# A Fourier filter with a gated feed-forward layer on one core: the gated layers worked unit by unit, PSUM dealt out as four, two and two banks, and another order of the work on ACT and DVE

## The chip, the core and the metric

The kernel runs on one core of one Trainium2 chip. The core has five engines with instruction queues of their own, each worked strictly in the order in which it was written: PE (matrix products, with PEld for the loading of weights), DVE, ACT and POOL (elementwise work), and SP, which here only issues DMAs. [...] The metric is the device time of one execution in microseconds (us), as the median of the runs shown. "Profiled execution" is one further run, from which the trace comes.

## The reference, cut to what matters

```python
X = np.fft.rfft(x, axis=1)                  # x: 8 batches, 3136 positions, 256 channels, fp32
Y = X * (filt_r + 1j * filt_i)[None, :, :]
x = np.fft.irfft(Y, n=3136, axis=1)
h = np.maximum(x @ w_in, 0.0)               # w_in 256 x 1024
hp = h padded by one position on either side
conv = sum(conv_w[k] * hp[:, k:k + 3136, :] for k in range(3))   # three taps per hidden channel
out = (h * 1.0 / (1.0 + np.exp(-conv))) @ w_out                  # w_out 1024 x 256
```

So each batch goes through a forward transform, a product with a filter, a backward transform, a matrix product with ReLU, a convolution of three taps, a sigmoid gate, and a second matrix product.

## The kernel before, in words

**The transform of a batch** is split as 3136 = 112 x 28 and runs in four kinds of operation, called "1" to "4" here as in the code, each of them 14 times per batch (two of the 28 columns at a time). "1" and "3" are products with a table that differs from column to column (`by_column`, L231), whose result ACT copies out of PSUM (`store`, L226) and SP sends to a scratch buffer in HBM. "2" is a product with a fixed matrix (`second`, L235), whose result DVE takes out of PSUM while multiplying it by the filter (`filt`, L244 to L246, three instructions of DVE), after which POOL adds the two halves (L247); the sum `z` is the input of a "3". "4" is the last product (`fourth`, L255, eight matmuls), whose result DVE copies to SBUF (L572), ACT rounds to the reduced format that PE takes at full rate (`y`, high part, L145), and POOL subtracts to have the low part (L151). Every "2" and "4" first loads what "1" and "3" wrote to HBM.

**The gated layers** are tiled by 448 positions (seven to a batch, 56 in all; the after-code calls such a tile a unit) and by 128 hidden channels (eight blocks `f`). For one tile and one block there are: `inner` (six matmuls of 450 columns, high and low parts, into a PSUM bank `ps_h`, L176 to L178); `relu` on ACT, in place in PSUM (L426), and the centre tap on ACT, from PSUM into an SBUF tile `t` (L428); the two outer taps on DVE, PSUM and `t` into `t` (`conv`, L433 and L434); the sigmoid on ACT (L438) and the product with h on DVE (`gate`, L439); the rounding of the gated value on ACT (L145) and its low part on POOL (`split_g`, L151); and `project`, three matmuls of 256 columns for each 128 positions, which add up over the eight blocks in PSUM banks `po` (L459 to L461). When the last block has been added, DVE copies `po` to SBUF (`evacuate`, L475) and SP stores it.

**What sets the order.** Batch 0's whole transform and batch 1's "1" come first, while the weights are converted (stage 1). Then stage 2 runs through 448 steps, one for each tile and block, by a loop in which everything on PE, ACT, DVE and POOL is issued in the order in which it is written. In step m stand the inner product of item m, the elementwise work of items m-1 to m-3, and the projection of item m-6. A table `plan` says in which steps one (or two) of the transform operations of the following batches stand. In the loop before, the operation is multiplied in the middle of the step on PE, and its result is taken out of PSUM at the very end of the same step on ACT or DVE (`transformed`):

```python
for op in ops[0:1]: transform(op)      # PE, behind inner(m)
project(m - 6); relu(m - 1); conv(m - 1); gate(m - 2); split_g(m - 3); evacuate(m - 6)
for op in ops: transformed(op)         # ACT, DVE, POOL
```

Before, tiles are worked in pairs of 896 positions with the two halves taking turns (seven groups of 128 positions to a pair: four in the first half, three in the second), so that four banks of `po` fill together; three banks serve `ps_h`, and one serves all transform operations (`ps_t`).

Of the kernel before, what the change touches and what calls it, by code (L numbers as in the profile page):

```python
# [124 lines left out]
def tile_fft_filter_gated_ffn(  # L125
# [18 lines left out]
    def hi_act(dst, src):  # L144
        nc.scalar.activation(dst, src, AF.Copy)  # L145
# [4 lines left out]
    def lo_pool(dst, src, hi):  # L150
        nc.gpsimd.tensor_tensor(out=dst, in0=src, in1=hi.bitcast(F32), op=ALU.subtract)  # L151
# [23 lines left out]
    def mm3(ps, wh, wl, rh, rl, start=True, stop=True, **kw):  # L175
        nc.tensor.matmul(ps, lhsT=wh, rhs=rh, start=start, stop=False, **kw)  # L176
        nc.tensor.matmul(ps, lhsT=wh, rhs=rl, start=False, stop=False, **kw)  # L177
        nc.tensor.matmul(ps, lhsT=wl, rhs=rh, start=False, stop=stop, **kw)  # L178
# [37 lines left out]
    def pair(q):  # L216
        return slice(2 * q, 2 * q + 2)
# [39 lines left out]
    def as_y(p):  # L257
        return p.rearrange("p (k c a) -> p k c a", c=2, a=N1)
# [150 lines left out]
    hs, ts, gs, pos = {}, {}, {}, {}  # L409

    def at(m):

        return (m // 16, m // 2 % NF, m % 2) if 0 <= m < 16 * (B * S // CH) else None

    def inner(j, f, i):
        ps = ps_h.tile([128, 512], F32, name="ps_h")[:, 0:SUB + 2]
        fs = slice(128 * f, 128 * f + 128)
        b, u = divmod(2 * j + i, NSUB)
        us = slice(u * SUB, u * SUB + SUB + 2)
        for k in range(KT):  # L420
            mm3(ps, wi[0][:, k, fs], wi[1][:, k, fs], ys[b][0][:, k, us], ys[b][1][:, k, us], start=k == 0, stop=k == KT - 1)
        hs[j, f, i] = ps

    def relu(j, f, i):
        h = hs[j, f, i]
        nc.scalar.activation(h, h, AF.Relu)  # L426
        t = wp.tile([128, SUB], F32, name="t", bufs=4)
        nc.scalar.activation(t, h[:, 1:SUB + 1], AF.Copy, scale=cw[:, 1, f:f + 1])  # L428
        ts[j, f, i] = t

    def conv(j, f, i):
        h, t = hs[j, f, i], ts[j, f, i]
        nc.vector.scalar_tensor_tensor(out=t, in0=h[:, 0:SUB], scalar=cw[:, 0, f:f + 1], in1=t, op0=ALU.mult, op1=ALU.add)  # L433
        nc.vector.scalar_tensor_tensor(out=t, in0=h[:, 2:SUB + 2], scalar=cw[:, 2, f:f + 1], in1=t, op0=ALU.mult, op1=ALU.add)  # L434

    def gate(j, f, i):
        h, t = hs.pop((j, f, i)), ts[j, f, i]
        nc.scalar.activation(t, t, AF.Sigmoid)  # L438
        nc.vector.tensor_mul(t, h[:, 1:SUB + 1], t)  # L439

    def split_g(j, f, i):
        t = ts.pop((j, f, i))
        if i == 0:
            gs[j, f] = [wp.tile([128, 2 * SUB], F32R, name=f"g{h}", bufs=3) for h in range(2)]
        gh, gl = (g[:, i * SUB:i * SUB + SUB] for g in gs[j, f])
        hi_act(gh, t)
        lo_pool(gl, t, gh)

    def project(j, f, i):
        gh, gl = gs[j, f]  # L450
        if f == 0 and i == 0:
            pos[j] = [ps_o.tile([128, 512], F32, name=f"po{k}") for k in range(4)]
        po = pos[j]
        tiles = range(4) if i == 0 else range(4, NT)
        for t in tiles:
            o = po[t // 2][:, t % 2 * D:t % 2 * D + D]
            sl = slice(128 * t, 128 * t + 128)
            first, last = f == 0 and t % 2 == 0, f == NF - 1
            nc.tensor.matmul(o, lhsT=gh[:, sl], rhs=wo[0][:, f], start=first, stop=False, skip_group_check=True)  # L459
            nc.tensor.matmul(o, lhsT=gh[:, sl], rhs=wo[1][:, f], start=False, stop=False, skip_group_check=True)  # L460
            nc.tensor.matmul(o, lhsT=gl[:, sl], rhs=wo[0][:, f], start=False, stop=last, skip_group_check=True)  # L461

    def evacuate(j, f, i):
        if f < NF - 1:
            return
        po = pos[j]
        end = j == B * S // CH - 1
        for k in (0, 1) if i == 0 else (2, 3):
            n = min(2, NT - 2 * k)
# [6 lines left out]
            nc.sync.dma_start(out=outv[j][:, 2 * k:2 * k + n], in_=ot[:, 0:n])  # L476

    NH = 16 * (B * S // CH)
    plan = {}

    def put(m, kind, b, q):
        plan.setdefault(m, []).append((kind, b, q))

    early = {}
    for t in range(1, B):
        w, n = (NF * NSUB * (t - 1), 49) if t % 2 else (NF * NSUB * (t - 1) - 7, 63)
        at2 = 4 if t == 1 else 0 if t % 2 else 10
        late = range(at2 + 34, n - 1)
        taken = set()
        for q in range(NP):  # L490
            at4 = late[q * len(late) // NP]
            taken |= {at2 + 2 * q, at2 + 3 + 2 * q, at4}
            put(w + at2 + 2 * q, "2", t, q)
            put(w + at2 + 3 + 2 * q, "3", t, q)
            put(w + at4, "4", t, q)
        free = [s for s in range(n if t % 2 else n - 4) if s not in taken]
        for q in range(early.get(t, NP), NP):
            put(w + free.pop(0), "1", t, q)
        if t + 1 < B:
            early[t + 1] = min(NP, len(free))  # L500
            if not t % 2:
                free = sorted(free + free[:NP - len(free)])
                early[t + 1] = NP
# [6 lines left out]
    got_in, got_table, got_filter, got_z, banks = {}, {}, {}, {}, {}  # L510

    stored = {("1", 1): NP}

# [45 lines left out]
        if kind == "4":  # L559
            fourth(ps, r)  # L560

    def transformed(op):
        kind, b, q = op
        ps = banks.pop(op)
        if kind in "13":
            store(tp, kind, b, q, ps, 3, "st")
            stored[kind, b] = stored.get((kind, b), 0) + 1
        if kind == "2":
            got_z[b, q] = filt(ps, q, got_filter.pop(op))
        if kind == "4":  # L570
            v = tp.tile([128, 2, D], F32, name="z", bufs=3).rearrange("p j d -> p (j d)")[:, 0:4 * N1]
            nc.vector.tensor_copy(v, ps[:, 0:4 * N1])  # L572
            yh, yl = y_slices(b, pair(q))
            hi_act(yh, as_y(v))
            lo_pool(yl, as_y(v), yh)

    with tc.manual_schedule(engines=COMPUTE):
        for m in range(NH + PLAG):
            ops = plan.get(m, [])
            if a := at(m):  # L580
                inner(*a)
            for op in ops[0:1]:
                transform(op)
            if a := at(m - PLAG):
# [58 lines left out]
```

## Time and profile before

| | us |
|---|---|
| median of 3 runs | 1829.6 (1828.79 to 1830.1) |
| profiled execution | 1823.64 |
| its span, first to last instruction | 1821.9 |
| PE busy in the span | 1586.1 (87%) |
| DVE busy | 1242.6 (68%) |
| ACT busy | 1179.6 (65%) |
| POOL busy | 819.7 (45%) |

The mean granted clock of PE is 0.972. A busy PE is not a PE at its peak, since matmuls overlap and their ends are modelled; the distance from one matmul's start to the next one's is the better measure. Stage 1 ends at about 152 us, where the first `inner` starts; the 448 steps fill the rest. Since each step has exactly two instructions of line L176, the number of these in a stretch of time gives its number of steps. The last 56 steps (batch 7) have no transform work.

### The profile page before, as it was taken

How to read it: one execution, taken by the hardware profiler on the slowest of the kernel's cores; microseconds unless marked ns; L12 is line 12 of the kernel's file. 1: busy time of each engine (PE TensorE's matmuls, PEld its weight loads, DVE VectorE, ACT ScalarE, POOL GpSimd, SP SyncE). 2: the span in 40 equal slices, each digit the busy share in tenths (PEclk: the TensorE clock that was granted, in tenths of full speed). 3: DMA queues.
4: the chain of work that ended last, by engine and by line, in shares of the span. 5: the costliest groups of instructions: out<-in, count | busy, mean ns of one | idle time of the engine just before them, and what ended most of it. 6: DMA issues, size and time to landing. Idle time of an engine off the chain costs nothing. (4 is left out here: it accounts for less than half of the span.)

```text
span 1821.9 us, 27328 instructions
## 1 busy us (share of the span) xinstructions
PE 1586.1 (87%) x9424; PEld 1380.1 (76%) x9424; DVE 1242.6 (68%) x1965; ACT 1179.6 (65%) x2176; POOL 819.7 (45%) x722
## 2 busy tenths in 40 slices
PE   4658998899887999799998899889998889978998
PEld 2347788787777778687887788778778777868998
DVE  0966875568755886558765688556785588757786
ACT  3337666666666666675666666667667666667887
POOL 0542444434444444534444454453444544454444
PEclk7769999999999999999999999999999999999999
DMA  9767553475421554155552355326553245210001
GB/s 281 211 198 238 160 157 121 123 215 165 125 70 45 171 169 139 59 174 170 152 153 85 103 166 161 111 73 202 161 170 105 86 134 155 73 51 21 21 21 41
DMA packets 171481, 238.64 MB, mean 131 GB/s; under 512 B 16696, under 2 KB 119121, under 8 KB 171345
## 3 DMA queue, kind: packets, MB, share of 16 engines
q1 hardware_dynamic: 171345, 236.92, 43.5%
q8 instruction: 75, 1.23, 0.3%
q14 instruction: 61, 0.50, 0.1%
HBM read 159.78 MB, written 77.07 MB: 130 GB/s over the span
## 5 line engine op out<-in xcount | busy, mean ns | idle before, releaser
L151 POOL TENSOR_TENSOR g<-t,g 128x448 fp32r<-128x448 f32 x448 | 514.8, 1149 | 534.2 <-issue 231.9
L433 DVE SCALAR_TENSOR_TENSOR t<-ps_h,cw,t 128x448 f32<-128x448 f32 x448 | 306.0, 683 | 459.7 <-ACT t L428 455.7
L459 PE MATMUL po<-wo,g 128*128 128x256 f32 x1568 | 517.9, 330 | 0.0
L176 PE MATMUL ps_h<-y,wi 128*128 128x450 f32 x896 | 345.0, 385 | 118.5 <-DVE t L439 116.9
L460 PE MATMUL po<-wo,g 128*128 128x256 f32 x1568 | 440.0, 281 | 0.0
L461 PE MATMUL po<-wo,g 128*128 128x256 f32 x1568 | 439.3, 280 | 0.0
L177 PE MATMUL ps_h<-y,wi 128*128 128x450 f32 x896 | 331.2, 370 | 0.6 <-DVE y L148 0.6
L178 PE MATMUL ps_h<-y,wi 128*128 128x450 f32 x896 | 329.3, 368 | 0.0
L459 PEld LDWEIGHTS po<-wo,g 128*128 128x128 f32 x1568 | 298.6, 190 | 31.0 <-issue 22.4
L460 PEld LDWEIGHTS po<-wo,g 128*128 128x128 f32 x1568 | 298.6, 190 | 27.7 <-issue 21.7
L434 DVE SCALAR_TENSOR_TENSOR t<-ps_h,cw,t 128x448 f32<-128x448 f32 x448 | 306.4, 684 | 16.0
L428 ACT ACTIVATE t<-ps_h,cw 128x448 f32<-128x448 f32 x448 | 285.0, 636 | 42.0 <-ACT ps_h L426 0.7
L226 ACT ACTIVATE st<-ps_t 112x512 f32<-112x512 f32 x182 | 108.9, 598 | 299.0 <-PE ps_t L231 299.0
L461 PEld LDWEIGHTS po<-wo,g 128*128 128x128 f32 x1568 | 298.6, 190 | 0.0
L176 PEld LDWEIGHTS ps_h<-y,wi 128*128 128x128 f32 x896 | 169.3, 189 | 149.3 <-DVE t L439 139.8
L439 DVE TENSOR_TENSOR t<-ps_h,t 128x448 f32<-128x448 f32 x448 | 275.1, 614 | 0.1
L426 ACT ACTIVATE ps_h<-ps_h 128x450 f32<-128x450 f32 x448 | 250.5, 559 | 31.3 <-PE ps_h L178 29.4
L247 POOL TENSOR_TENSOR z<-z,v 120x512 f32<-120x512 f32 x112 | 146.3, 1306 | 266.4 <-DVE v L246 266.4
L438 ACT ACTIVATE t<-t 128x448 f32<-128x448 f32 x448 | 254.6, 568 | 1.3 <-DVE t L434 1.2
L145 ACT ACTIVATE g<-t 128x448 fp32r<-128x448 f32 x448 | 253.7, 566 | 0.1
L145 ACT ACTIVATE y<-z 128x448 fp32r<-128x448 f32 x98 | 104.5, 1066 | 169.6 <-DVE z L572 169.6
L151 POOL TENSOR_TENSOR y<-z,y 128x448 fp32r<-128x448 f32 x98 | 137.6, 1404 | 158.3 <-ACT y L145 158.3
(66 smaller groups left out, 1670.6 us busy)
## 6 DMA issues: line engine op xcount, KB each, us to landing
filt<-in_filt SPq DMA_DIRECT2D x98, 512.0 KB, 3.6
tin<-a_dram SPq DMA_DIRECT2D x98, 224.0 KB, 2.6
b_dram<-st SPq DMA_DIRECT2D x98, 224.0 KB, 3.0
tin<-b_dram SPq DMA_DIRECT2D x98, 224.0 KB, 2.7
out<-ot SPq DMA_DIRECT2D x84, 256.0 KB, 2.4
tin<-in_x SPq DMA_DIRECT2D x84, 224.0 KB, 2.6
a_dram<-st SPq DMA_DIRECT2D x84, 224.0 KB, 3.0
tab<-in_i SPq DMA_DIRECT2D x98, 105.0 KB, 3.0
```

Source lines behind the costliest of these rows:

```text
L145: nc.scalar.activation(dst, src, AF.Copy)
L151: nc.gpsimd.tensor_tensor(out=dst, in0=src, in1=hi.bitcast(F32), op=ALU.subtract)
L176: nc.tensor.matmul(ps, lhsT=wh, rhs=rh, start=start, stop=False, **kw)
L177: nc.tensor.matmul(ps, lhsT=wh, rhs=rl, start=False, stop=False, **kw)
L178: nc.tensor.matmul(ps, lhsT=wl, rhs=rh, start=False, stop=stop, **kw)
L428: nc.scalar.activation(t, h[:, 1:SUB + 1], AF.Copy, scale=cw[:, 1, f:f + 1])
L433: nc.vector.scalar_tensor_tensor(out=t, in0=h[:, 0:SUB], scalar=cw[:, 0, f:f + 1], in1=t, op0=ALU.mult, op1=ALU.add)
L434: nc.vector.scalar_tensor_tensor(out=t, in0=h[:, 2:SUB + 2], scalar=cw[:, 2, f:f + 1], in1=t, op0=ALU.mult, op1=ALU.add)
L439: nc.vector.tensor_mul(t, h[:, 1:SUB + 1], t)
L459: nc.tensor.matmul(o, lhsT=gh[:, sl], rhs=wo[0][:, f], start=first, stop=False, skip_group_check=True)
L460: nc.tensor.matmul(o, lhsT=gh[:, sl], rhs=wo[1][:, f], start=False, stop=False, skip_group_check=True)
L461: nc.tensor.matmul(o, lhsT=gl[:, sl], rhs=wo[0][:, f], start=False, stop=last, skip_group_check=True)
```

## The change

The stages, the operations on PE and their number stay. Five things differ in stage 2:

1. **Unit by unit.** The eight blocks of one tile of 448 positions are worked one after another, and then those of the next. A tile has three whole groups of 128 positions and half a group (64); the half group of an even unit is kept for all eight blocks in eight small tiles `gm` and is completed and projected with the odd unit. Rounding and low part therefore become two instructions each, of 384 and 64 columns, instead of one of 448.
2. **Two `po` banks** hold a unit's sums (three groups for even units, four for odd), and are copied out after eight steps; before, four banks were copied out in the last two of 16 steps. The number of copies and stores stays 112.
3. **Four banks for `ps_h`, two for `ps_t`.** `g` tiles now have 384 columns and four buffers (before: 896 columns, three). `t` keeps its four buffers, but is read one step longer, since the low part moves from step m+3 to step m+4.
4. **Order within a step.** The result of a transform operation is taken out of its bank in the step after the one in which PE made it, on DVE as the first thing of that step, on ACT between `relu` and the centre tap. For "4", rounding to `y` stands behind the rounding of `g`, and its low part on POOL behind that of `g`. The taps and the gate on DVE now run tap 0, gate of the item before, tap 2.
5. **The plan.** It is the same for each batch: in the 56 steps of a batch there are "1" in steps 0 to 3; "2" in every even step from 4 to 30 and "3" in every odd step from 7 to 33, with "1" in 5 and 32; "1" in 34 to 36; "4" in steps 37 to 52, but for two steps with a "1"; in three of these steps (50 to 52) there is a "4" and a "1"; and steps 53 to 55 have none.

The core of the diff (the unchanged arithmetic inside the moved functions is left out):

```diff
-    ps_h = ctx.enter_context(tc.tile_pool(name="ps_h", bufs=3, space=bass.MemoryType.PSUM, reuse_waits="tile"))
-    ps_t = ctx.enter_context(tc.tile_pool(name="ps_t", bufs=1, space=bass.MemoryType.PSUM, reuse_waits="tile"))
+    ps_h = ctx.enter_context(tc.tile_pool(name="ps_h", bufs=4, space=bass.MemoryType.PSUM, reuse_waits="tile"))
+    ps_t = ctx.enter_context(tc.tile_pool(name="ps_t", bufs=2, space=bass.MemoryType.PSUM, reuse_waits="tile"))
...
+    def round_g(u, f):
+        gs[u, f] = [wp.tile([128, 384], F32R, name=f"g{h}", bufs=4) for h in range(2)]
+        if u % 2 == 0:
+            mids[u // 2, f] = [wp.tile([128, 128], F32R, name=f"gm{h}", bufs=NF) for h in range(2)]
+        for g, o, i in split_parts(u, f):
+            hi_act(g[0][:, o], ts[u, f][:, i])
+
+    def rest_g(u, f):
+        for g, o, i in split_parts(u, f):
+            lo_pool(g[1][:, o], ts[u, f][:, i], g[0][:, o])
+        del ts[u, f]
...
-            pos[j] = [ps_o.tile([128, 512], F32, name=f"po{k}") for k in range(4)]
+            pos[u] = [ps_o.tile([128, 512], F32, name=f"po{k}") for k in range(2)]
...
     with tc.manual_schedule(engines=COMPUTE):
-        for m in range(NH + PLAG):
-            ops = plan.get(m, [])
+        for m in range(NF * NU + PLAG):
+            p1, p2, p3, p4, p6 = (at(m - k) for k in (1, 2, 3, 4, PLAG))
+            new, old = plan.get(m, []), plan.get(m - 1, [])
             if a := at(m):
                 inner(*a)
-            for op in ops[0:1]:
+            if p1:
+                relu(*p1)
+            for op in old:
+                from_bank(op)
+            want_in()
+            for op in new:
                 transform(op)
...
+            if p1:
+                centre(*p1)
+            if p2:
+                sigmoid(*p2)
+            if p1:
+                tap(*p1, 0)
+            if p3:
+                round_g(*p3)
+            later = [to_y(op) for op in old]
+            if p2:
+                gate(*p2)
+            if p4:
+                rest_g(*p4)
+            if p6:
+                project(*p6)
+            for step in later:
+                step()
+            if p1:
+                tap(*p1, 2)
+            if p6:
+                evacuate(*p6)
```

**Steps with a "4".** On ACT (first batch of stage 2; the numbers behind the names count buffers, so that one name is followed from engine to engine), before:

```order
L145 ACTIVATE y0_2375<-z_2428 128x2x2x112
L426 ACTIVATE ps_h_2396<-ps_h_2396 128x450
L428 ACTIVATE t_2459<-ps_h_2396,cw_79 128x448
L438 ACTIVATE t_2418<-t_2418 128x448
L145 ACTIVATE g0_2424<-t_2365 128x448
L145 ACTIVATE y0_2375<-z_2467 128x2x2x112
```

And on DVE, before, where the copy out of the "4" bank (L572) is the last thing of a step:

```order
L572 COPY z_2428<-ps_t_2403 128x448
L433 SCALAR_TENSOR_TENSOR t_2459<-ps_h_2396,cw_79,t_2459 128x448
L434 SCALAR_TENSOR_TENSOR t_2459<-ps_h_2396,cw_79,t_2459 128x448
L439 TENSOR_TENSOR t_2418<-ps_h_2336,t_2418 128x448
L572 COPY z_2467<-ps_t_2441 128x448
```

Before, the copy to `z_2467` stands behind both taps and the gate of a step whose centre tap `t_2459` ACT makes only after `y` of the "4" before it (from `z_2428`).

Now ACT and, below it, DVE have in the same place:

```order
L145 ACTIVATE y0_4873<-z_4856 128x2x2x112
L427 ACTIVATE ps_h_4848<-ps_h_4848 128x450
L431 ACTIVATE t_4916<-ps_h_4848,cw_79 128x448
L438 ACTIVATE t_4865<-t_4865 128x448
L145 ACTIVATE g0_4920<-t_4821 128x384
L145 ACTIVATE gm0_4587<-t_4821 128x64
L145 ACTIVATE y0_4873<-z_4907 128x2x2x112
```

```order
L576 COPY z_4907<-ps_t_4860 128x448
L435 SCALAR_TENSOR_TENSOR t_4916<-ps_h_4848,cw_79,t_4916 128x448
L441 TENSOR_TENSOR t_4865<-ps_h_4803,t_4865 128x448
L435 SCALAR_TENSOR_TENSOR t_4916<-ps_h_4848,cw_79,t_4916 128x448
L576 COPY z_4950<-ps_t_4911 128x448
```

The copy to `z_4907` now stands ahead of the taps of `t_4916`, and so ahead of everything that waits for the centre tap of its own step.

**Steps with a "2" and a "3" in turn.** POOL, before, had per two steps one sum `z` and two low parts of 448 columns:

```order
L247 TENSOR_TENSOR z_3519<-z_3519,v1_87 120x512
L151 TENSOR_TENSOR g1_3516<-t_3477,g0_3515 128x448
L151 TENSOR_TENSOR g1_3590<-t_3509,g0_3589 128x448
L247 TENSOR_TENSOR z_3593<-z_3593,v0_86 120x512
L151 TENSOR_TENSOR g1_3590<-t_3551,g0_3589 128x448
```

And now one sum and four low parts:

```order
L247 TENSOR_TENSOR z_4225<-z_4225,v1_87 120x512
L151 TENSOR_TENSOR g1_4196<-t_4108,g0_4195 128x384
L151 TENSOR_TENSOR gm1_3872<-t_4108,gm0_3871 128x64
L151 TENSOR_TENSOR g1_4242<-t_4149,g0_4241 128x384
L151 TENSOR_TENSOR gm1_3917<-t_4149,gm0_3916 128x64
L247 TENSOR_TENSOR z_4308<-z_4308,v0_86 120x512
```

The items that follow `t_4108` are `t_4149`, `t_4191`, `t_4237` and `t_4276`; with four buffers, the centre tap that writes `t_4276` takes the buffer that POOL frees with the low parts of `t_4108`, and these now stand behind the sum `z_4225`. DVE has in this place:

```order
L244 TENSOR_TENSOR z_4225<-ps_t_4187,filt_4105 120x512
L245 TENSOR_TENSOR v1_87<-ps_t_4187,filt_4105 56x512
L246 SCALAR_TENSOR_TENSOR v1_87<-ps_t_4187,filt_4105 56x512
L435 SCALAR_TENSOR_TENSOR t_4237<-ps_h_4176,cw_79,t_4237 128x448
L441 TENSOR_TENSOR t_4191<-ps_h_4129,t_4191 128x448
L435 SCALAR_TENSOR_TENSOR t_4237<-ps_h_4176,cw_79,t_4237 128x448
L435 SCALAR_TENSOR_TENSOR t_4276<-ps_h_4217,cw_79,t_4276 128x448
L441 TENSOR_TENSOR t_4237<-ps_h_4176,t_4237 128x448
L435 SCALAR_TENSOR_TENSOR t_4276<-ps_h_4217,cw_79,t_4276 128x448
L244 TENSOR_TENSOR z_4308<-ps_t_4272,filt_4188 120x512
```

The filter's three instructions now open every second step, and between those of `z_4225` and of `z_4308` stand two steps' taps and gates, the second of which begins with a tap of `t_4276`.

More of the change, by code (lines that the diff above doesn't have):

```diff
@@ L416, in inner @@
+    def inner(u, f):
         ps = ps_h.tile([128, 512], F32, name="ps_h")[:, 0:SUB + 2]
         fs = slice(128 * f, 128 * f + 128)
-        b, u = divmod(2 * j + i, NSUB)
-        us = slice(u * SUB, u * SUB + SUB + 2)
+        yh, yl = ys[u // NSUB]
+        us = slice(u % NSUB * SUB, u % NSUB * SUB + SUB + 2)
         for k in range(KT):
[L421 to L447, printed above, removed]
@@ L449, in project @@
-    def project(j, f, i):
-        gh, gl = gs[j, f]
-        if f == 0 and i == 0:
-            pos[j] = [ps_o.tile([128, 512], F32, name=f"po{k}") for k in range(4)]
[L453 to L457, printed above, removed]
+            mm3(ps, wi[0][:, k, fs], wi[1][:, k, fs], yh[:, k, us], yl[:, k, us], start=k == 0, stop=k == KT - 1)
+        hs[u, f] = ps
@@ new lines, in relu, with centre, tap, sigmoid @@
+    def relu(u, f):
+        nc.scalar.activation(hs[u, f], hs[u, f], AF.Relu)
+    def centre(u, f):
+        ts[u, f] = t = wp.tile([128, SUB], F32, name="t", bufs=4)
+        nc.scalar.activation(t, hs[u, f][:, 1:SUB + 1], AF.Copy, scale=cw[:, 1, f:f + 1])
+    def tap(u, f, k):
+        h, t = hs[u, f], ts[u, f]
+        nc.vector.scalar_tensor_tensor(out=t, in0=h[:, k:SUB + k], scalar=cw[:, k, f:f + 1], in1=t, op0=ALU.mult, op1=ALU.add)
+    def sigmoid(u, f):
+        nc.scalar.activation(ts[u, f], ts[u, f], AF.Sigmoid)
@@ new lines, in gate, with split_parts @@
+    def gate(u, f):
+        nc.vector.tensor_mul(ts[u, f], hs.pop((u, f))[:, 1:SUB + 1], ts[u, f])
+    def split_parts(u, f):
+        if u % 2:
+            return ((gs[u, f], slice(0, 384), slice(HALF, SUB)), (mids[u // 2, f], slice(HALF, 128), slice(0, HALF)))
+        return ((gs[u, f], slice(0, 384), slice(0, 384)), (mids[u // 2, f], slice(0, HALF), slice(384, SUB)))
+    def round_g(u, f):
[4 more added lines that the diff above has]
+            hi_act(g[0][:, o], ts[u, f][:, i])
@@ new lines, in rest_g, with project @@
+    def rest_g(u, f):
+        for g, o, i in split_parts(u, f):
+            lo_pool(g[1][:, o], ts[u, f][:, i], g[0][:, o])
+        del ts[u, f]
+    def project(u, f):
+        g = gs.pop((u, f))
+        tiles = [[h[:, 128 * k:128 * k + 128] for h in g] for k in range(3)]
+        if u % 2:
+            tiles = [[h[:] for h in mids.pop((u // 2, f))]] + tiles
+        if f == 0:
+            pos[u] = [ps_o.tile([128, 512], F32, name=f"po{k}") for k in range(2)]
+        for t, (gh, gl) in enumerate(tiles):
+            o = pos[u][t // 2][:, t % 2 * D:t % 2 * D + D]
@@ L458, in project @@
             first, last = f == 0 and t % 2 == 0, f == NF - 1
[L459 to L463, printed above, removed]
+            nc.tensor.matmul(o, lhsT=gh, rhs=wo[0][:, f], start=first, stop=False, skip_group_check=True)
@@ L464, in evacuate @@
+            nc.tensor.matmul(o, lhsT=gh, rhs=wo[1][:, f], start=False, stop=False, skip_group_check=True)
+            nc.tensor.matmul(o, lhsT=gl, rhs=wo[0][:, f], start=False, stop=last, skip_group_check=True)
+    def evacuate(u, f):
         if f < NF - 1:
             return
[L466 to L469, printed above, removed]
+        t0, nt = (3, 4) if u % 2 else (0, 3)
+        for k in range(2):
+            n = min(2, nt - 2 * k)
@@ L470, in evacuate @@
             ot = wp.tile([128, 2, D], F32, name="ot", bufs=3)
-            o, src = ot[:, 0:n].rearrange("p t d -> p (t d)"), po[k][:, 0:n * D]
-            if end and k % 2:
+            o, src = ot[:, 0:n].rearrange("p t d -> p (t d)"), pos[u][k][:, 0:n * D]
+            if u == NU - 1 and k:
                 nc.scalar.activation(o, src, AF.Copy)
@@ L475, in evacuate @@
                 nc.vector.tensor_copy(o, src)
-            nc.sync.dma_start(out=outv[j][:, 2 * k:2 * k + n], in_=ot[:, 0:n])
-    NH = 16 * (B * S // CH)
+            nc.sync.dma_start(out=outv[u // 2][:, t0 + 2 * k:t0 + 2 * k + n], in_=ot[:, 0:n])
+    NW = NF * NSUB
     plan = {}
@@ L482, in put @@
         plan.setdefault(m, []).append((kind, b, q))
-    early = {}
     for t in range(1, B):
[L486 to L489, printed above, removed]
+        w = NW * (t - 1)
+        at2, at4 = 4, [37 + 17 * q // NP for q in range(NP)]
+        used = set(at4)
         for q in range(NP):
-            at4 = late[q * len(late) // NP]
-            taken |= {at2 + 2 * q, at2 + 3 + 2 * q, at4}
+            used |= {at2 + 2 * q, at2 + 3 + 2 * q}
             put(w + at2 + 2 * q, "2", t, q)
             put(w + at2 + 3 + 2 * q, "3", t, q)
[L495 to L498, printed above, removed]
+            put(w + at4[q], "4", t, q)
+        free = [s for s in range(53) if s not in used]
+        free = sorted(free + [s for s in range(0, 53) if s // NF % 2 == 0 and s not in free][::-1][:NP - len(free)])
         if t + 1 < B:
[L500 to L503, printed above, removed]
             for q, s in enumerate(free[:NP]):
@@ L509, in tile_fft_filter_gated_ffn @@
     filters = [op for _, op in order if op[0] == "2"]
-    got_in, got_table, got_filter, got_z, banks = {}, {}, {}, {}, {}
+    got_in, got_table, got_filter, got_z, banks, vs = {}, {}, {}, {}, {}, {}
     stored = {("1", 1): NP}
```

34 lines of the change are left out of this document (12 added, 22 removed).

## The prediction

> **What bounds the kernel now.** I read the page first (span, busy shares: no engine is full), then the busy time of line L176 by stretches, since two L176 make one step, and then the chain of waits inside the stretches that are slow. The columns are from:to, length, PE busy on L176 with its count, granted clock, DMA share and rate.
>
> ```profile
> 152.45:371.40 218.95, 43.91 (x113) 0.99 0.52 154
> 1026.85:1243.53 216.68, 42.83 (x112) 1.00 0.46 137
> 1049.25:1099.05 49.80, 10.35 (x28) 1.00 0.55 162
> 1148.90:1215.75 66.85, 11.64 (x28) 1.00 0.23 71
> 1220.52:1243.53 23.01, 5.22 (x14) 1.00 0.66 198
> 1711.42:1740.42 29.00, 8.77 (x24) 1.00 0.00 1
> 1670.90:1821.90 151.00, 41.56 (x112) 1.00 0.08 25
> ```
>
> Stage 2 starts at 152.45 and a batch of 56 steps takes about 217. The fourth to last rows within it are: "2" and "3" in turn, 49.80 / 14 = 3.557 a step (7.11 a pair); steps with a "4", 66.85 / 14 = 4.775; steps with a "1", 23.01 / 7 = 3.287; steps with no operation (last batch), 29.00 / 12 = 2.417. In the last two kinds PE waits for nothing to speak of, so an operation is worth 3.287 - 2.417 = 0.87 of PE. I take 0.87 for all four kinds. So a "4" step costs 4.775 where PE needs 3.287, and a pair 7.11 where it needs 6.57. What takes the rest is shown by the chain of waits, first in the "4" steps:
>
> ```profile
> 1384.30 1.09 ACT y L145
> 1385.39 0.43 ACT ps_h L426
> ...
> 1385.91 0.64 ACT t L428
> ...
> 1388.51 0.54 DVE z L572
> ...
> 1389.08 1.07 ACT y L145
> ```
>
> PE isn't in it. It is a ring of ACT and DVE: y waits for the copy L572, which stands behind both taps and the gate; the taps wait for the centre tap, which stands behind the y before. One turn, 1389.08 - 1384.30 = 4.78, is the step. In the pairs the ring goes through the one transform bank:
>
> ```profile
> 1519.03 1.10 PE ps_t L231 x4
> ...
> 1520.15 0.60 ACT st L226
> ...
> 1521.28 0.64 ACT t L428
> ...
> 1525.19 0.70 DVE v L246
> ...
> 1526.14 1.09 PE ps_t L231 x4
> ```
>
> A "3" on PE, its copy on ACT, the centre tap behind it, taps, gate and filter on DVE, and only then is the bank free for the next "3": 7.11 again.
>
> **The change part by part.** *"4" steps.* The copy now stands ahead of the taps on DVE and y behind the rounding on ACT, so the ring is cut: y waits for a copy that needs only PE's result and the step before. What is left is each engine's own work, and PE's 3.287 is the most: on DVE a copy, two taps and a gate are about 0.6 + 1.8, on ACT see below. Gain 4.775 - 3.287 = 1.49 on each.
>
> *Rounding in two pieces.* ACT's spacing over one step, and DVE's and POOL's, come from the timeline (start, length):
>
> ```profile
> 474.33 0.61 DVE L439 TENSOR_TENSOR t<-ps_h,t 128x448 f32<-128x448 f32 x1
> 474.86 0.68 DVE L244 TENSOR_TENSOR z<-ps_t,filt 120x512 f32<-120x512 f32 x1
> 476.25 0.69 DVE L246 SCALAR_TENSOR_TENSOR v<-ps_t,filt 56x512 f32<-56x512 f32 x1
> 477.02 1.27 POOL L247 TENSOR_TENSOR z<-z,v 120x512 f32<-120x512 f32 x1 [1.84 <-DVE v L246]
> 477.69 0.68 DVE L434 SCALAR_TENSOR_TENSOR t<-ps_h,cw,t 128x448 f32<-128x448 f32 x1
> 478.25 1.16 POOL L151 TENSOR_TENSOR g<-t,g 128x448 fp32r<-128x448 f32 x1
> 478.29 0.61 DVE L439 TENSOR_TENSOR t<-ps_h,t 128x448 f32<-128x448 f32 x1
> 478.82 0.54 ACT L426 ACTIVATE ps_h<-ps_h 128x450 f32<-128x450 f32 x1
> 480.97 0.53 ACT L426 ACTIVATE ps_h<-ps_h 128x450 f32<-128x450 f32 x1
> ```
>
> ```profile
> L151 POOL TENSOR_TENSOR g<-t,g 128x448 fp32r<-128x448 f32 x448 | 514.8, 1149 | 534.2 <-issue 231.9 <-ACT g L145 221.3 <-PE ps_h L178 41.5
> L145 ACT ACTIVATE g<-t 128x448 fp32r<-128x448 f32 x448 | 253.7, 566 | 0.1
> L151 POOL TENSOR_TENSOR wo<-ws,wo 128x256 fp32r<-128x256 f32 x8 | 6.7, 839 | 0.0
> L145 ACT ACTIVATE wo<-ws 128x256 fp32r<-128x256 f32 x8 | 3.2, 400 | 0.0
> L428 ACT ACTIVATE t<-ps_h,cw 128x448 f32<-128x448 f32 x448 | 285.0, 636 | 42.0 <-ACT ps_h L426 0.7 <-POOL g L151 0.4
> L173 POOL TENSOR_TENSOR cw<-cw,em 128x24 f32<-128x24 f32 x1 | 0.2, 233 | 12.0 <-DVE em L171 12.0
> ```
>
> ACT takes 480.97 - 478.82 = 2.15 a step. Its slope is (566 - 400) / 192 = 0.86 ns a column, so 448 columns in two pieces cost the constant part again, 566 - 387 = 0.18: 2.33, still under PE's 2.417; with y (1.09) 3.42 if nothing overlaps, and the chain shows relu only 0.43 long behind y's end where it lasts 0.54 in the timeline, so about 3.3, as much as PE. It is the tightest place, and its cover is two steps of bank depth. POOL: slope (1149 - 839) / 192 = 1.61, so 384 columns take 1.05, and 64 columns between 0.30 (by the row of 24 columns) and 0.53 (by the line through 256 and 448); I take 0.33, near the 24-column row. Both pieces, 1.38; a "4" step has 1.38 + about 1.4 for y's low part, under 3.287.
>
> *The pair's new ring.* Two transform banks free PE: a "2" needs the bank of the "2" two steps ago. But t keeps four buffers while its last reader moved one step later, behind the sum z. So: filter on DVE; sum on POOL; low parts on POOL; centre tap on ACT, which takes the buffer set free; tap 0, gate, tap 2 on DVE; the next filter. Price: L244's start to the end of the sum, 478.25 - 474.86 = 3.39; low parts 1.38 less 0.04 of overlap between neighbours; a hand-over of 0.07 (L246's end at 476.94 to 477.02); the centre tap with its hand-over 0.64 + 0.04; two taps and a gate at 0.60 from start to start (477.69 to 478.29), 1.80 at most and 1.73 if what follows the gate starts 0.53 later, as at 474.33 to 474.86; I take 1.73. Sum: 3.39 + 1.34 + 0.07 + 0.68 + 1.73 = 7.21 a pair. With POOL's ends 7.18 to 7.41; if the sequence closes over more than two steps it is no bound at all and PE's 6.57 is. So the pairs hardly gain over 7.11; PE waits there, for the bank and for ps_h.
>
> *Two po banks.* Copies are needed every 8 steps instead of 16, two at a time, 2 x 0.62 = 1.24 of DVE. In the pairs DVE is idle from the last tap until the next tap 0 (1.34 + 0.07 + 0.68 + 1.31 of sum, less 1.73, is 1.67), and the copies fall in just that step: nothing. Elsewhere they end before PE has done the next inner product: nothing. Without this cover it costs 56 x 1.24 = 69. In exchange the four-bank stops go: the last batch's 55 steps are 136.9 now (to 1807.8) against 55 x 2.417 = 132.9.
>
> *DMA.* Every load and store stays, 112 output stores too. Loads are asked for half a step earlier, behind the copies out of the bank, and SP waits there for ACT's copies as before; the share of 0.23 to 0.66 leaves room at a pace a tenth faster. I cost it at nothing; a late load would cost one step's idling each.
>
> **The sum.** A batch of 56 steps: 22 single steps x 3.287 = 72.3; 3 with two operations x (2.417 + 1.74) = 12.5; 3 bare, 7.3; 14 pairs x 7.21 = 100.9; together 193.0, against 217. Six of these, 1158. The seventh has no "1": 13 bare 31.4, 15 single 49.3, pairs 100.9, together 181.6. The last, 151.0 - 4.0 = 147.0. With 152.45 ahead: 1639 for the span of 1821.9. The profiled execution lies 1.7 over its span, at 1823.64, and the median of the runs 0.33% over that, so **1639 becomes 1646**.
>
> **Rivals.** *Pairs at PE's pace* (the new ring doesn't close): 98 x (7.21 - 6.57) = 63 less, 1583. For it: four buffers may free earlier than I think; against it, the rows of POOL and ACT stand in just that order. *The two po banks stop PE at each unit*: up to 69 more, 1715. For it: before, such stops appear at each emptying; against, DVE has the time. *The "4" ring isn't cut*, because y still waits for something of its own step: 98 x 1.49 = 146 more, 1792; against it stands the order of copy and taps. The slower side: *PE's clock drops*.
>
> ```profile
> 80.00:120.00 40.00, 20.81 (x50) 12.79 (x51) 29.62 (x42) 11.30 (x23) 19.83 (x21) 0.63 0.69 210
> ```
>
> Here (columns PE, PEld, DVE, ACT, POOL, clock) PE is half idle and its granted clock 0.63, while in all rows of stage 2 above it is 0.99 or 1.00, with pauses too. Were it to fall with the new changing of banks, a batch's PE time would grow: PE needs about 56 x 2.417 + 56 x 0.87 = 184, and at 0.84 it is 219 a batch, as before; from there on the kernel is slower, and at 0.63 a batch is 292, the total near 2420. [...]
>
> **How the numbers follow.** Forecast 0.70 (its own range 1620 to 1685: POOL's ends give 1643 to 1666, ACT's tightness in the "4" steps up to 0.2 x 98 = 20 more, PE ahead of the ring a little less); pairs at PE's pace 0.10; po stops 0.14, mostly in part; "4" ring uncut 0.03; clock 0.03. The range 1600 to 1710 leaves out the "4" ring, the clock, the whole po stop and most of the first rival: two in ten. This kernel's runs tell 0.2% from no change; all cases but the last are faster by more than that, and of the uncut ring I count a third as same.
>
> **What would show it.** In the changed kernel: "4" steps near 3.3 with PE and no ring of ACT and DVE in the chain; pairs near 7.2 with the centre tap L431 waiting for POOL's L151, and DVE's tap waiting for L431; bare steps at 2.42; few waits of PE's L459 line for the copies of po. I'd be wrong if pairs are near 6.6 or above 7.5, if "4" steps stay above 3.6, or if PE waits for DVE at unit ends.

## The result, and the profile of the changed kernel

| | before | changed |
|---|---|---|
| median, us | 1829.19 (1824.88 to 1830.1, 4 runs) | 1621.46 (1618.95 to 1624.88, 4 runs) |
| ratio | 1 | 0.887, 95% interval 0.8848 to 0.8892 |
| span of the profiled execution, us | 1821.9 | 1618.9 |
| sum of the prediction for the span, us | | 1639 |

The change makes the kernel 11.3% faster. The forecast of 1646 had the direction, the places and the range right; it is 25 us (1.5%) too high. The rival in which the pairs run at PE's pace (1583) is 38 us too low, so the result lies between the two.

The head of the page of the changed kernel, the shares of the chain of waits, and the groups that carry the reading (line, engine, operation, tiles, count | busy us, mean ns of one | idle before it, and what ended that):

```profile
span 1618.9 us, 28466 instructions
...
PE 1527.6 (94%) x9424; PEld 1363.0 (84%) x9424; DVE 1203.6 (74%) x1966; ACT 1202.6 (74%) x2623; POOL 878.3 (54%) x1170
...
PE 73%; issue 9%; DVE 6%; POOL 6%; DMA 3%; ACT 2%; SPq 1%; POOLq 0%; DVEq 0%; ACTq 0%
...
L151 POOL TENSOR_TENSOR g<-t,g 128x384 fp32r<-128x384 f32 x448 | 455.1, 1016 | 182.5 <-ACT g L145 72.8
L431 ACT ACTIVATE t<-ps_h,cw 128x448 f32<-128x448 f32 x448 | 284.9, 636 | 231.1 <-POOL gm L151 206.2
...
L151 POOL TENSOR_TENSOR gm<-t,gm 128x64 fp32r<-128x64 f32 x448 | 145.9, 326 | 0.0
```

PE is now busy for 94% of the span (87% before) with the same 9424 matmuls. ACT sat idle for 231.1 us before the centre tap L431, and 206.2 of that ended with POOL's low part `gm`: the wait for a free `t` that the prediction named. The low parts take 1016 and 326 ns; the prediction had estimated 1.05 and 0.33 us.

Steps by stretches, as before the change (from:to, length, PE busy on L176 with its count, two to a step, granted clock, DMA share and rate):

```profile
1103.15:1115.65 12.50, 2.92 (x8) 1.00 0.48 137
659.00:701.82 42.82, 9.57 (x26) 1.00 0.40 115
847.95:891.68 43.73, 9.49 (x26) 1.00 0.39 114
544.05:641.50 97.45, 20.65 (x56) 1.00 0.57 173
1549.30:1597.00 47.70, 14.61 (x40) 1.00 0.06 20
1472.00:1618.90 146.90, 40.90 (x112) 1.00 0.08 26
```

In this order: steps with a "1", 12.50 / 4 = 3.13; thirteen steps with a "4" each but for two with a "1", of an even and of an odd batch, (42.82 + 43.73) / 26 = 3.33 (before 4.775); 28 steps with "2" and "3" in turn (one of them has a "1" in the place of a "3"), 97.45, or 6.96 a pair (before 7.11); bare steps, 47.70 / 20 = 2.39 (before 2.417); and the last batch, 146.9 (before 151.0). The first six batches take 189.9 on the average (152.05 to 1291.30); before, they took 218.5 (152.51 to 1463.32), which is 28.6 more. Of these, by the stretches shown, 14 x (4.775 - 3.33) = 20 are in the "4" steps, 14 x (7.11 - 6.96) = 2 in the pairs, and 6 in all the others, with the stops at the old four-bank copies.

In the "4" steps the ring of ACT and DVE is gone. DVE (first fence) and ACT (second) at one "4", from the timeline (start, length, idle time before and what ended it):

```profile
688.69 0.62 DVE L576 COPY z<-ps_t 128x448 f32<-128x448 f32 x1
690.93 0.62 DVE L576 COPY z<-ps_t 128x448 f32<-128x448 f32 x1
691.60 0.68 DVE L435 SCALAR_TENSOR_TENSOR t<-ps_h,cw,t 128x448 f32<-128x448 f32 x1
```

```profile
689.34 1.07 ACT L145 ACTIVATE y<-z 128x448 fp32r<-128x448 f32 x1 [0.69 <-DVE z L576]
...
691.93 0.52 ACT L145 ACTIVATE g<-t 128x384 fp32r<-128x384 f32 x1
692.35 0.25 ACT L145 ACTIVATE gm<-t 128x64 fp32r<-128x64 f32 x1
692.50 1.03 ACT L145 ACTIVATE y<-z 128x448 fp32r<-128x448 f32 x1
```

From one `y` to the next is 692.50 - 689.34 = 3.16, the pace of PE, and the second `y` waits for nothing: the copy it needs, at 690.93, was made ahead of the taps and had ended 0.95 before. The first waited 0.69 for its copy, which stood on DVE behind a copy of `po` (688.36).

In the pairs the ring of the prediction runs. One turn of it in the timeline:

```profile
603.45 0.68 DVE L244 TENSOR_TENSOR z<-ps_t,filt 120x512 f32<-120x512 f32 x1
605.62 1.29 POOL L247 TENSOR_TENSOR z<-z,v 120x512 f32<-120x512 f32 x1 [3.34 <-DVE v L246]
606.86 1.00 POOL L151 TENSOR_TENSOR g<-t,g 128x384 fp32r<-128x384 f32 x1
607.82 0.32 POOL L151 TENSOR_TENSOR gm<-t,gm 128x64 fp32r<-128x64 f32 x1
608.18 0.64 ACT L431 ACTIVATE t<-ps_h,cw 128x448 f32<-128x448 f32 x1 [2.32 <-POOL gm L151]
608.85 0.68 DVE L435 SCALAR_TENSOR_TENSOR t<-ps_h,cw,t 128x448 f32<-128x448 f32 x1 [0.28 <-ACT t L431]
610.57 0.68 DVE L244 TENSOR_TENSOR z<-ps_t,filt 120x512 f32<-120x512 f32 x1
```

Filter, sum, two low parts, centre tap, tap, and 610.57 - 603.45 = 7.12 later the next filter (7.21 predicted). And yet 28 steps take 97.45 here, not 14 x 7.12 = 99.7. PE's "2" and DVE's filter, at the first and at the thirteenth pair of this batch, show how:

```profile
545.29 1.02 PE L235 MATMUL ps_t<-tin,s_sb 112*120 112x512 f32 x2
627.00 1.09 PE L235 MATMUL ps_t<-tin,s_sb 112*120 112x512 f32 x2 [0.60 <-PE ps_h L178]
```

```profile
546.35 0.69 DVE L244 TENSOR_TENSOR z<-ps_t,filt 120x512 f32<-120x512 f32 x1 [0.50 <-PE ps_t L235]
631.94 0.68 DVE L244 TENSOR_TENSOR z<-ps_t,filt 120x512 f32<-120x512 f32 x1
```

The filters are (631.94 - 546.35) / 12 = 7.13 apart, the "2" on PE (627.00 - 545.29) / 12 = 6.81. DVE follows PE at 1.06 us at the first pair and at 4.94 at the thirteenth: PE runs ahead on the free banks, and DVE makes the delay good in the steps without a "2", where it has less to do. Only what the banks don't hold stops PE, and it stops where it next needs something of DVE. The waits over the whole execution (engine, line, waited for: us in total, times, longest):

```profile
ACT t L431 <- POOL gm L151: 206.2, 103, 2.4
PEld po L471 <- DVE ot L486: 27.4, 17, 2.1
PEld ps_t L235 <- PE ps_h L178: 11.6, 13, 1.0
PEld ps_t L238 <- PE ps_h L178: 3.7, 4, 0.9
```

The first is 206 us of waiting on ACT that costs the span a fraction of it. The second is PE at the first projection of a unit, waiting for DVE to copy `po` out. L235 and L238 are the "2"; the profile puts their wait down to PE's own product, which had ended, and what ended just before is the filter of the "2" two steps earlier, whose bank they take. Together 42.7 us in 34 waits, a first measure of what the ring costs. These are waits of PE's weight loads (PEld), part of which passes under a matmul that is still running; the rows of PE itself have 15.7, 7.0 and 2.3 for the same three, 25.0 in all.

### The profile page after: what moved, and what is told of

Its sections match the earlier page's. It is cut to its first block, busy times and chain, and to the rows that moved or that the text cites. A ratio compares the mean times of both kernels' runs of the same rounds, so it can differ in the third digit from the quotient of the medians.

```text
span 1618.9 us, 28466 instructions
## 1 busy us (share of the span) xinstructions
PE 1527.6 (94%) x9424; PEld 1363.0 (84%) x9424; DVE 1203.6 (74%) x1966; ACT 1202.6 (74%) x2623; POOL 878.3 (54%) x1170
## 4 chain that ended last, share of the span: by engine, by line
PE 73%; issue 9%; DVE 6%; POOL 6%; DMA 3%; ACT 2%; SPq 1%; POOLq 0%; DVEq 0%; ACTq 0%
PE po L471 10%; PE po L472 9%; PE po L473 9%; PE ps_h L177 9%; PE ps_h L178 9%; PE ps_h L176 9%; PE ps_t L231 8%; PE ps_t L255 5%; POOL g L151 4%; PE ps_t L235 2%; DVE t L435 2%; POOL gm L151 1%; DMA a_dram<-sa 1%; DVE v L246 1%; DVE v L245 1%
## 5 line engine op out<-in xcount | busy, mean ns | idle before, releaser
L151 POOL TENSOR_TENSOR g<-t,g 128x384 fp32r<-128x384 f32 x448 | 455.1, 1016 | 182.5 <-ACT g L145 72.8
L431 ACT ACTIVATE t<-ps_h,cw 128x448 f32<-128x448 f32 x448 | 284.9, 636 | 231.1 <-POOL gm L151 206.2
L471 PE MATMUL po<-wo,g 128*128 128x256 f32 x1344 | 413.5, 308 | 1.9 <-DVE ot L486 1.9
L473 PE MATMUL po<-wo,g 128*128 128x256 f32 x1344 | 374.4, 279 | 0.0
L472 PE MATMUL po<-wo,g 128*128 128x256 f32 x1344 | 374.2, 278 | 0.0
L176 PE MATMUL ps_h<-y,wi 128*128 128x450 f32 x896 | 330.8, 369 | 1.2 <-ACT y L145 1.2
L177 PE MATMUL ps_h<-y,wi 128*128 128x450 f32 x896 | 330.2, 369 | 0.6 <-DVE y L148 0.6
L178 PE MATMUL ps_h<-y,wi 128*128 128x450 f32 x896 | 328.3, 366 | 0.0
L471 PEld LDWEIGHTS po<-wo,g 128*128 128x128 f32 x1344 | 253.6, 189 | 21.2 <-issue 9.9
L472 PEld LDWEIGHTS po<-wo,g 128*128 128x128 f32 x1344 | 253.5, 189 | 13.4 <-issue 10.3
L473 PEld LDWEIGHTS po<-wo,g 128*128 128x128 f32 x1344 | 253.7, 189 | 0.0
L145 ACT ACTIVATE g<-t 128x384 fp32r<-128x384 f32 x448 | 231.9, 518 | 10.4 <-PE po L472 9.7
L178 PEld LDWEIGHTS ps_h<-y,wi 128*128 128x128 f32 x896 | 168.8, 188 | 14.2
L176 PEld LDWEIGHTS ps_h<-y,wi 128*128 128x128 f32 x896 | 169.6, 189 | 9.4 <-issue 1.6
L177 PEld LDWEIGHTS ps_h<-y,wi 128*128 128x128 f32 x896 | 169.1, 189 | 7.8 <-issue 1.1
L151 POOL TENSOR_TENSOR gm<-t,gm 128x64 fp32r<-128x64 f32 x448 | 145.9, 326 | 0.0
```

The source lines that it names most:

```text
L431: nc.scalar.activation(t, hs[u, f][:, 1:SUB + 1], AF.Copy, scale=cw[:, 1, f:f + 1])
L471: nc.tensor.matmul(o, lhsT=gh, rhs=wo[0][:, f], start=first, stop=False, skip_group_check=True)
L472: nc.tensor.matmul(o, lhsT=gh, rhs=wo[1][:, f], start=False, stop=False, skip_group_check=True)
L473: nc.tensor.matmul(o, lhsT=gl, rhs=wo[0][:, f], start=False, stop=last, skip_group_check=True)
```

## The experiments

The theory to test: the gain comes from the order in the "4" steps; in the pairs the ring through four `t` buffers sets DVE's pace, and the second transform bank lets PE absorb most of its delay. Rivals: PE's waits for `po` are the price of only two `po` banks, and not of the ring; the gain comes from the tiling and the banks, and the order only adds to it; the second bank is worth nothing by itself. The experiments are edits of the changed kernel, except one of the kernel before. Ratios are to the kernel before, on the same chip.

**Does the ring close through the `t` buffers?** A fifth buffer opens it, and a third less closes it over fewer steps:

```diff
-        ts[u, f] = t = wp.tile([128, SUB], F32, name="t", bufs=4)
+        ts[u, f] = t = wp.tile([128, SUB], F32, name="t", bufs=5)
```

> The changed kernel with five buffers for t instead of four. My theory: in the steps with a '2' and a '3' in turn, DVE's filters are 7.12 us apart because of a ring filter, sum on POOL, low parts on POOL, centre tap on ACT (which waits for the buffer), taps and gate on DVE; with a fifth buffer the centre tap waits for low parts of one step earlier, the ring is open, and the pairs fall to PE's own pace, 6.6 a pair. The 28 steps of pairs of a batch, 97.3 now, become 92 to 93, so 7 x 4.8 = 34 us less: 1587 (1580 to 1600). Rival: the 7.12 is the work of DVE itself or the loading of filters, and a buffer changes nothing: 1621.

Measured 1584.0 us (1583.25 to 1584.63), ratio 0.8675 (0.866 to 0.8691). The page's head, and 28 steps of pairs in an even and an odd batch:

```profile
span 1582.4 us, 28502 instructions
```

```profile
531.10:623.40 92.30, 20.66 (x56) 1.00 0.63 186
716.50:810.00 93.50, 20.44 (x56) 1.00 0.61 182
```

The pairs take 92.3 to 93.5, 6.6 each, PE's own pace. All else being the same, the spans differ by 1618.9 - 1582.4 = 36.5, and that is the price of the ring in the changed kernel. The waits that concern PE's meeting with DVE, now:

```profile
PEld po L471 <- DVE t L435: 4.5, 18, 0.2
PEld po L471 <- DVE ot L486: 0.2, 1, 0.2
```

PE's 27.4 us of waiting for `po` are gone with the same two `po` banks. So these were the ring's delay showing at another place: without that delay what is left of such waits is 4.7 us in 19, none over 0.2. Whether a third `po` bank would have held the delay with the ring in place was not tried.

```diff
-        ts[u, f] = t = wp.tile([128, SUB], F32, name="t", bufs=4)
+        ts[u, f] = t = wp.tile([128, SUB], F32, name="t", bufs=3)
```

> The changed kernel with three buffers for t instead of four, so that the suspected wait gets worse: the centre tap of a step now waits for the low parts issued in the same step. My theory: every ring closes one step earlier. Bare steps 3.1 us instead of 2.42 (rounding, low parts 1.34, centre tap, sigmoid, rounding); steps with a '4' about 5.5 instead of 3.3 (y, its low part, the low parts of g, the centre tap, then y again); pairs 9.4 to 9.9 instead of 7.12. Total about 1621 + 38 + 210 + 225 = 2095 (1950 to 2150). Rival, that the buffers of t are not on the path: under 1640.

Measured 2137.96 us (two runs, 2137.34 and 2138.57), ratio 1.171 (1.1685 to 1.1735). Waits of this kernel, and a stretch of 28 steps of pairs in it:

```profile
ACT t L431 <- POOL gm L151: 838.3, 440, 5.1
```

```profile
679.45:817.30 137.85, 23.04 (x56) 0.90 0.41 123
```

Now the centre tap waits in 440 of 448 steps. The fourteen filters stand 10.06 apart (from 681.8 to 812.6), and the pairs take 137.85 / 14 = 9.85. The expectation had 9.4 to 9.9 between filters, slightly too little; the total lies within its range. With one buffer less the kernel is slower than before the change, in both of the two runs: three, four and five buffers give 2138, 1621 and 1584 us.

**The same ring cut at another place.** Here the buffers stay four, but POOL makes the low parts ahead of the sum, and so frees `t` earlier:

```diff
+            if p4:
+                rest_g(*p4)
             for op in old:
                 from_bank(op)
...
-            if p4:
-                rest_g(*p4)
```

> The changed kernel with the two low-part instructions of g moved ahead of the filter's sum in POOL's order of a step; t keeps four buffers. My theory: the ring through POOL opens just as with a fifth buffer, since the low parts no longer stand behind the sum of the same step: DVE's filters come down from 7.12 apart to PE's 6.6, total 1587 (1580 to 1605). Rival, that POOL is simply late there or that the buffer count alone decides: 1615 to 1625.

Measured 1585.49 us (1582.58 to 1586.86), ratio 0.8682 (0.8668 to 0.8696), and for 28 steps of pairs:

```profile
532.15:624.45 92.30, 20.66 (x56) 1.00 0.62 186
```

This is the fifth buffer's result without a fifth buffer. Two edits that share only the ring give the same 92.30, so it is POOL's order together with the number of `t` buffers that cost the 36 us, and not PSUM, DMA or memory.

**What makes the "4" steps faster?** Here tiling, banks and the order of the taps stay as changed, but the result of an operation is taken out at the end of its own step, as before:

```diff
-            for op in old:
-                from_bank(op)
-            want_in()
...
-            later = [to_y(op) for op in old]
...
-            for step in later:
-                step()
...
+            for op in new:
+                from_bank(op)
+                to_y(op)()
+                want_in()
```

> The changed kernel with one part undone: the result of a transform operation is again taken out of its bank, and y and its low part made, at the end of the step in which PE makes it; tiling, banks (four, two, two), pieces of g and order of taps stay as changed. My theory: the ring of y, centre tap, taps, gate, copy is back, so '4' steps take 4.7 (0.98 + 0.63 + 0.68 + 1.73 + 0.6), while pairs stay near 7.1: 98 x 1.4 = 137 more, about 1758 (1730 to 1800). Rival, that the gain comes from more PSUM banks: under 1660.

Measured 1760.94 us (1760.45 to 1763.24), ratio 0.9647 (0.9632 to 0.9663). The old ring is back, from one `y` to the next on ACT:

```profile
715.24 1.04 ACT L145 ACTIVATE y<-z 128x448 fp32r<-128x448 f32 x1 [1.38 <-DVE z L576]
...
719.85 1.04 ACT L145 ACTIVATE y<-z 128x448 fp32r<-128x448 f32 x1 [1.38 <-DVE z L576]
```

One turn is 719.85 - 715.24 = 4.61, against 3.16 in the changed kernel, and each `y` again waits for the copy of its own step. Taking the results out a step later is worth 1761 - 1621 = 140 us of the 208. That this is so near 98 x (4.775 - 3.33) = 142 is luck, for not every "4" step takes 4.61 here. The thirteen steps from step 37 of a batch on (first line) and the six behind them up to the batch's end, three with two operations and three bare (second line), and, in the second fence, those six in the changed kernel, where the thirteen took 42.82:

```profile
701.00:754.72 53.72, 10.53 (x26) 0.97 0.28 88
754.72:781.74 27.02, 4.54 (x12) 1.00 0.41 124
```

```profile
701.82:722.06 20.24, 4.41 (x12) 1.00 0.53 155
```

The thirteen steps are 53.72 / 13 = 4.13 long: the first ones still go at PE's pace, the next at the ring's, and in some PE stops for longer. Of the 19 us that this batch is longer, 11 are in these steps, 7 in the six behind them and the rest in the pairs (98.92 against 97.45). The granted clock is lower too: 0.955 on the mean over the span of 1761.3 us, in the changed kernel 0.974 over 1618.9. By an estimate from these numbers, up to 0.045 x 1761.3 - 0.026 x 1618.9 = 37 of the 140 us can be the slower clock. How much of it is was not separated.

**How much does the order alone give?** The kernel before, with its tiling in pairs, four `po` banks, three `ps_h`, one `ps_t` and one rounding of 448 columns, but with the changed order within a step (the loop is written out here in short; the low part of `g` stays in step m+3, so that `t` is free earlier than in the change, and of two operations in a step the first is taken out in it):

```diff
-for op in ops[0:1]: transform(op)
-project(m - 6); relu(m - 1); conv(m - 1); gate(m - 2); split_g(m - 3); evacuate(m - 6)
-for op in ops: transformed(op)
+relu(m - 1); from_bank(old); transform(new); centre(m - 1); sigmoid(m - 2); tap(m - 1, 0)
+round_g(m - 3); gate(m - 2); rest_g(m - 3); project(m - 6); low part of y; tap(m - 1, 2); evacuate(m - 6)
```

> The kernel before with one part of the change alone: the order within a step (results taken out one step later, ahead of the taps on DVE and behind relu on ACT, y behind the rounding, tap 0, gate, tap 2). Tiling in pairs of 896, four banks of sums, three for the inner product, one for the transform, the plan and one rounding of 448 columns stay as before. My theory: most of the gain is there: '4' steps near 3.3 instead of 4.78, and pairs, whose low parts still run one step earlier so that the ring through t doesn't close, between 6.6 and 7.1; the stops at the emptying of four banks remain. 1610 to 1680. Rival, that the gain needs the new banks and units: over 1740.

Measured 1640.03 us (1636.66 to 1646.22), ratio 0.8987 (0.8962 to 0.9012). Thirteen steps with a "4" each, and 28 steps of pairs:

```profile
666.75:710.50 43.75, 9.53 (x26) 1.00 0.32 97
745.30:846.60 101.30, 20.46 (x56) 1.00 0.58 172
```

The "4" steps are at 43.75 / 13 = 3.37. So the order gives 1826.23 - 1640.03 = 186 us, nine tenths of what the whole change gives (208); tiling, banks and plan, which this kernel has as before, give the rest, about 20. They would give more without the ring through `t`, which this kernel doesn't have: 1640 - 1584 = 56. In the pairs most steps take 3.15 to 3.80, but one or two in each batch 5.0 to 6.4 us (7.3 and 9.3 in batch 1); that these are the stops at the emptying of four `po` banks is read from their place, every 16 steps, and was not tried by itself.

**What is the second transform bank worth?** One `ps_t` and five `ps_h`; where a step has two operations, the first is taken out within the step:

```diff
-    ps_h = ... bufs=4
-    ps_t = ... bufs=2
+    ps_h = ... bufs=5
+    ps_t = ... bufs=1
...
-            new, old = plan.get(m, []), plan.get(m - 1, [])
+            new, old = plan.get(m, []), plan.get(m - 1, [])[-1:]
...
-            for op in new:
+            for op in new[:1]:
                 transform(op)
...
+            for first, op in zip(new, new[1:]):
+                from_bank(first)
+                to_y(first)()
+                transform(op)
```

> The changed kernel with one bank for the transform operations and five for the inner product, instead of two and four; where a step has two operations, the first is taken out in the same step. The rest, the order above all, stays. My theory: order is what counts; with one bank PE must wait in the pairs for DVE's filter, which comes every 7.12, so a lag can't be absorbed any more: 28 steps of pairs about 100 instead of 97, '4' steps 3.3 to 3.6: 20 to 60 us more, 1640 to 1680. Rival, that the second transform bank is the main gain: '4' steps near 4.7 again, over 1740.

Measured 1651.56 us (1650.43 to 1654.45), ratio 0.9048 (0.9028 to 0.9069). Pairs, and the thirteen steps with "4" and two "1":

```profile
553.68:653.42 99.74, 20.69 (x56) 1.00 0.59 173
670.85:714.35 43.50, 9.55 (x26) 1.00 0.39 113
```

The pairs take 99.74 / 14 = 7.12, exactly the ring's pace: with one bank PE can't run ahead. That is the term of the prediction as it stood there (7.21), and it is right for this kernel. The thirteen steps take 43.50 / 13 = 3.35, so the "4" steps don't need the second bank.

The same kernel with a fifth `t`, so that there is no ring to run ahead of:

> One transform bank and five for the inner product, and five buffers for t (the two edits of the earlier runs together, everything else as changed). With one bank alone the 28 steps of pairs took 99.5 us, with five buffers alone 92.4 to 93.5. My theory: the second bank's use in the pairs was to let PE run ahead of a ring that was slower than PE; with the ring open DVE is in time and one bank costs only the waits in which a filter of 2.1 us doesn't fit behind PE's projection and next inner product: pairs 93 to 97, and the steps with two operations some 2 us more a batch because one result is taken out in the same step: 1595 to 1625. Rival, that one bank bounds the pairs by itself (PE, filter, PE, copy in turn): pairs again near 99.5 and 1645 or more.

Measured 1626.17 us (1625.38 to 1627.46), ratio 0.8913 (0.8886 to 0.894), just above the expected range:

```profile
545.26:640.90 95.64, 20.67 (x56) 1.00 0.61 180
```

With the ring open, one bank still costs 1626.17 - 1584.0 = 42 us. In the pairs it is 95.64 - 92.30 = 3.3 in this batch, of about 6; the rest is mostly in the three steps with two operations, in this batch 4.17, 4.70 and 4.91 long in place of 4.35, and in those behind them. So the second bank does more than absorb the ring's delay, and the theory that this was its whole worth falls.

**The best kernel of these** is the changed one with five `t` buffers: 1584.0 us, 13% under the kernel before and 2.3% under the change. The low parts ahead of the sum do the same for no memory.

## Why the prediction was right, and what was off

*"4" steps: right.* Cutting the ring was to bring 4.775 to 3.287; measured 3.33, with 3.16 where PE projects three groups and 3.50 where it projects four. The rival that the ring stays is refuted by the `y` that waits for nothing, and its reason is shown by taking the results out in the same step, which brings it back.

*Single, double and bare steps: right.* 3.13 against 3.287 for "1", with three groups, and 3.47 with four; 4.03 and 4.35 against 4.157 for the steps with two operations; bare 2.39 against 2.417; the last batch 146.9 against 147.0. That the cost of an operation is the same for all four kinds held well enough for the sum.

*Two-piece rounding: right.* POOL at 1016 and 326 ns against 1050 and 330; ACT kept PE's pace in the "4" steps, its tightest place. The 330 was a choice between 300 and 530 that no row settled, and that it came out so well is partly luck.

*Pairs: the ring right, its effect mis-sized.* The step that failed is "14 pairs x 7.21 = 100.9" a batch. The ring turns in 7.12 to 7.13, but 28 steps take 97.4 on the average over the seven batches (96.7 to 98.8). Over seven batches the term is (100.9 - 97.4) x 7 = 24 us too high. All other terms together are 4 us too low, which leaves the 20 us between 1639 and the span of 1618.9; the other 5 of the 25 come from the step from the span to the median, for which the prediction added 7 and the runs show 2.6. A ring that leaves out PE set PE's pace here only where PE had used up its banks. The prediction also looked for PE's waits at the wrong place, "for the bank and for ps_h": the larger part, 27.4 us, is at `po`, 15.3 us are at the bank, and none of any size is for a bank of `ps_h`. The sum priced a pattern of 28 steps as if it went on for ever, while the delay that builds up in it, (7.13 - 6.6) x 14 = 7.4 us, is partly held by the banks and made good behind it: 36.5 / 7 = 5.2 us a batch are left of it. One bank less, and the same term is right, 99.74. Nor was it "no bound at all", as the lower end of the prediction had it: opened, the pairs take 92.30, and the whole kernel 1584, which was the time given for that rival (1583).

*Two `po` banks: the cost right, the sign to look for wrong.* The prediction costed them at nothing for DVE's idle time, and said that few PE waits for `po` would show it. There are 17, of 27.4 us. Read by themselves they would have spoken for the rival at 1715. But they go when the ring is opened, and what is left of these waits is 4.7 us in short pieces. DVE was late there because it had waited for ACT, and ACT for POOL.

*Clock: right for the sum.* Stage 2 has 0.99 or 1.00 in the stretches shown, and with a fifth buffer too. The kernel before has nine stretches of 3.41 us at 0.50 in its stage 2, 30.7 us against 7.6 in the changed kernel, so by an estimate that counts half of that time as lost at most (30.7 - 7.6) / 2 = 12 of the 208 us can be a clock that falls less often. That the clock would fall with the new changing of banks, as in the rival that the prediction gave 0.03, no run shows: with four, two and two banks in rotation the mean granted clock is 0.974, before it was 0.972. One stretch at 0.50 did occur in the middle of the changed kernel's stage 2, below.

## What to carry to other kernels

Where engines wait for one another in a ring, look first for the instruction that stands behind work of its own step, and move it ahead: that order alone was worth 186 us here, where the whole change gave 208. A ring that doesn't hold the bounding engine costs only what the buffers between them can't absorb over the length of the pattern, so compute its delay per batch and not its pace times the steps. And the engine that a wait is charged to may be the last in a line: before adding banks for it, open the ring upstream by one buffer, or by letting the work that frees a buffer go ahead of other work on that engine.

## What the runs showed of the hardware

In batch 3 of the changed kernel PE's granted clock was 0.50 for 3.41 us, behind a stretch of 3.41 us in which PE was busy for 0.44 of the time. By stretches (from:to, length, then PE, PEld, DVE, ACT and POOL with counts, clock, DMA share and rate), and PE in the timeline; the last two lines of the first fence are a place in batch 4 where PE stood still for less of the stretch:

```profile
795.53:798.94 3.41, 1.49 (x6) 0.68 (x6) 3.27 (x6) 1.11 (x3) 2.80 (x4) 1.00 0.51 123
798.94:802.35 3.41, 3.41 (x15) 3.28 (x15) 2.99 (x5) 3.32 (x9) 0.95 (x2) 0.50 0.91 303
1013.98:1017.39 3.41, 1.80 (x8) 0.96 (x6) 3.36 (x6) 1.49 (x4) 2.17 (x2) 1.00 0.33 71
1017.39:1020.81 3.42, 3.17 (x21) 2.98 (x22) 2.90 (x6) 2.95 (x7) 1.60 (x4) 1.00 0.83 297
```

```profile
798.55 0.38 PE L471 MATMUL po<-wo,gm 128*128 128x256 f32 x1 [1.30 <-DVE ot L486]
800.99 0.58 PE L176 MATMUL ps_h<-y,wi 128*128 128x450 f32 x1
```

PE was busy for 1.49 of 3.41 us (0.44), and for the next 3.41 us its clock is 0.50; a matmul of 450 columns takes 0.58 in place of 0.37. The two steps there are 6.83 and 4.13 long, where the same steps of batches 1 and 5 are 5.89 and 3.47: 1.6 us. In batch 4 PE was busy for 1.80 of 3.41 us (0.53), and the clock stayed at 1.00. The falls in stage 2 of this kernel, at 153.82, at 798.94 and, 0.8 us before the end of the span, at 1618.14, lie 189 and 240 times 3.4133 us apart; the nine in stage 2 of the kernel before last 3.41 us each and lie whole numbers of 3.4133 us apart too. If the stage 2 of each of these two kernels is cut into stretches of that length, counted from one of its falls, then PE is busy for under 0.45 of the time in ten stretches at full clock, and a fall followed each of them; of the eight with 0.47 to 0.49 it followed one (0.485, at 293.21 in the kernel before), and of those with more none. With three `t` buffers, where PE waits 101 times for DVE's gate (143.1 us in all) and 50 times for a copy of `po` (174.6 us), the granted clock is 0.90 over the 28 steps of pairs shown above and 0.899 over the span of 2135.6 us. By an estimate from that and the changed kernel's 0.974 over 1618.9, of the 517 us that it is slower than the change up to 0.101 x 2135.6 - 0.026 x 1618.9 = 174 can be the clock; how much is, and how much the ring alone, was not separated.

Of the rate of the rounded format the runs show this much: the products of `inner`, with rounded operands of 450 columns, start 0.20 to 0.21 us after one another (from 1103.17 on in the changed kernel), 0.46 ns a column; a "1", on fp32 tiles that are not rounded, costs 3.287 - 2.417 = 0.87 us of PE for 512 columns in the kernel before, 1.7 ns a column with the loading of its weights.
